# Four groups of products per step of a gated recurrence, with two shared PSUM banks in turn

## The chip, the cores and the metric

The kernel runs on one core of a Trainium2 chip. The metric is the device time of one execution in microseconds (us); smaller is better. The median of three runs of the kernel before is 412.56 us, the lowest 410.94, the highest 412.81.

## What is computed

A gated linear recurrence over 768 tokens for 4 batches of 8 heads, each 48 wide, is followed by a mixture of experts with one expert per token:

```python
f = 1.0 / (1.0 + np.exp(-f_logit))
for t in range(S):
    state = f[:, :, t, :, None] * state + np.einsum('bhd,bhe->bhde', k[:, :, t], v[:, :, t])
    y[:, :, t] = np.einsum('bhd,bhde->bhe', q[:, :, t], state)
x = y.transpose(0, 2, 1, 3).reshape(B * S, H * D)     # 3072 rows of 384
logits = x @ w_gate                                   # 8 experts
expert_idx = np.argmax(logits, axis=1)
gate_w = softmax(logits)[expert_idx]
out = gate_w * (relu(x @ w1[expert_idx]) @ w2[expert_idx])   # 384 -> 1024 -> 384
```

## The kernel before

The recurrence is computed in chunks of 128 tokens. A unit is one chunk of two batches (16 heads); there are 12 units, and units of the same parity follow one another in time for the same pair of batches. Everything is in float32. For each unit, `steps` (L446, lines 452 and 455) computes the log decays from f with Exp and Ln on ScalarE, `total` (L457) takes their running sum with a scan on VectorE, `growth` (L471) and `decay` (L485) take Exp of it with both signs on ScalarE, `by_r` (L478) multiplies the keys on GpSimd and `by_decay` (L497) the queries on VectorE.

On TensorE a unit then needs seven groups of products, which the loop over n at L721 writes out by hand, as a software pipeline over three units. In step n, with `here` = n, `back` = n - 1 and `last` = n - 2:

- `score(here, 0)` and `score(here, 1)` (L505): keys times queries, two heads side by side on 64 partitions each. `copy_predicated` on VectorE (L515) keeps the causal part.
- `keys(here)` (L517), between the two: turns the keys by products with the identity (tile kp), which `keep` (L527) copies to kn on ScalarE.
- `rows(last)` (L603): turns the results into rows and computes the logits in the same products (tile xp), reduced on VectorE (lg, L628). `settle` (L595) has copied those results out of yt, `lay` (L638) copies the rows on ScalarE, and waits for the reduction of the same bank.
- `within(back)` (L531): masked scores times v, accumulated in yt; `before(back)` (L546): the state times the queries, in the same yt.
- `added(here)` (L567): kn times v (tile dp), which `update` (L583) adds to the state on VectorE; GpSimd multiplies by the decay in the step after. Units 10 and 11 have no `added`, as nobody uses their state.

Every second step a group of two units is routed (class `Route`, L195): `choose` picks the expert on VectorE, `count` (L218) makes two products (tile rp), `place` (L223) turns the counts into rows of the sorted store xs in the next step, `weigh` and `fill` compute the gate and `send` scatters the rows with GpSimd's DMA queue.

The order of each engine's instructions is the order in which this code issues them (`manual_schedule`, L652); so each engine's queue, SyncE's with the loads included, goes in program order. [...]three for scores (pss), two for yt, and three (pst) which kp, xp, dp and rp share; the function `turns` (L413) names the bank for each so that each use has two or more uses of other banks ahead of its reuse. The first unit's step n = 0 has an order of its own (L744 to L768), with products of zeros (`warm`) that keep TensorE busy. Loads of k, q, v and f are issued at the end of each step, two to five units ahead. The buffer of f has two places, so f of unit u + 2 can only be loaded when `steps(u)` has read the place. In step 1 `load_first_pads` (L363) writes zeros to 288 rows of xs. In steps 8 and 10 the loads of the first two experts' weights follow.

Behind the recurrence, from step 12 on, the first 128 rows of two experts are read back and worked on while the last units are routed; then all eight experts are worked through (`widen` L295, `narrow` L318). That part is not touched.

Of the kernel before, what the change touches and what calls it, by code (L numbers as in the profile page):

```python
# [10 lines left out]
F32 = mybir.dt.float32  # L11
# [3 lines left out]
OP = mybir.AluOpType  # L15
# [97 lines left out]
def _bc(ap, axis, n):  # L113
    shape = list(ap.shape)
    shape.insert(axis, n)
    return ap[tuple([slice(None)] * axis + [None])].to_broadcast(shape)
# [3 lines left out]
def kernel(  # L120
# [262 lines left out]
    with ExitStack() as st:  # L383
        ld = st.enter_context(tc.tile_pool(name="ld", bufs=1))
        wk = st.enter_context(tc.tile_pool(name="wk", bufs=2))
        pss = st.enter_context(tc.tile_pool(name="pss", bufs=3, space=PSUM))
        psy = st.enter_context(tc.tile_pool(name="psy", bufs=1, space=PSUM))
# [20 lines left out]
        units = [{} for _ in range(NU)]  # L408
        states = [None, None]

        had, used = {"xp0": 0, "xp1": 1, "dp": 2, "rp": None}, [0, 1, 2]

        def turns(what, shape, steady=True):  # L413

            counts = had["rp"] is not None
            b = used[0]
            if steady:
                b = {
                    "kp0": had["dp"] if counts else had["xp0"],
                    "kp1": had["xp1"],  # L420
                    "xp0": had.get("kp0", 0),
                    "xp1": had["rp"] if counts else had.get("kp1", 1),
                    "dp": had.get("kp1", 1) if counts else had["dp"],
                    "rp": had["xp0"],
                }[what]
            had[what] = b
            if what == "dp":
                had["rp"] = None
            used.remove(b)
            used.append(b)  # L430
            return pst.tile(shape, F32, name=what, tag=f"tr{b}")

# [44 lines left out]

        def by_r(u, part=whole):  # L478
            k = units[u]["k"][:, part]
            nc.gpsimd.tensor_tensor(k, k, units[u]["r"][:, part], op=OP.mult)  # L480

# [23 lines left out]
        def score(u, a):  # L505
            x = units[u]
            x["at"] = scores[u % 2]
            ps = [pss.tile([128, HP, C], F32, name="s") for h in range(2)]
            for p, h, r in heads():
                s = HP * a + p  # L510
                nc.tensor.matmul(  # L511
                    ps[h][:, p], lhsT=x["k"][r, s], rhs=x["q"][r, s], start=True, stop=True
                )
            for h in range(2):
                nc.vector.copy_predicated(x["at"][:, a, h], _bc(causal, 1, HP), ps[h])  # L515

        def keys(u):  # L517
            x = units[u]
            x["kn"] = wk.tile([128, SEG, C], F32, name="kn", bufs=1)
            x["kp"] = []  # L520
            for a in range(2):
                kp = turns(f"kp{a}", [128, HP, C], u < NU - 2)
                for p in range(HP):
                    nc.tensor.transpose(kp[:, p], x["k"][:, HP * a + p], ident)  # L524
                x["kp"].append(kp)
# [69 lines left out]
        def settle(u):  # L595
            x = units[u]
            x["ys"] = wk.tile([128, 2, HP, C], F32, name="ys", bufs=1)
            for a in range(2):
                nc.scalar.copy(x["ys"][:, a], x["yt"][:, a])

        group = {}

        def rows(u):  # L603

# [11 lines left out]
            for a in range(2):  # L616
                j = 2 * (u - g[0]) + a
                xp = turns(f"xp{a}", [128, HP, XW], u < NU - 4)
                for p in range(HP):
                    nc.tensor.matmul(  # L620
                        xp[:, p],
                        lhsT=x["ys"][:, a, p],
                        rhs=wx[:, p, 0:XW] if a else wx[:, p, E:WX],
                        start=True,
                        stop=True,
                    )
                gate = slice(0, E) if a else slice(2 * D, XW)
                nc.vector.reduce_sum(  # L628
                    group["lg"][:, j],
                    xp[:, :, gate].rearrange("p h e -> p e h"),  # L630
                    axis=AX_X,
                )
                x["xp"].append(xp)
# [26 lines left out]
        for i in (1, 0):  # L660
            nc.gpsimd.memset(scores[i], 0.0)
        warmth = pst.tile([128, C], F32, name="warmth", tag="tr2")

        def warm(count):

            for _ in range(count):
                nc.tensor.matmul(warmth, lhsT=pad[:, 0:C], rhs=pad[:, 0:C], start=True, stop=True)  # L667

# [6 lines left out]
        for part in ab:  # L675
            growth(0, part)
            by_r(0, part)
            decay(0, part)
            by_decay(0, part)
# [18 lines left out]
        def narrow_early(x, w):  # L698
            narrow(x, 0, w, turns("yp", [128, DM], False), None)

# [19 lines left out]
        sends, later, decayed = [], None, None  # L720
        for n in range(NU + 2):  # L721
            here, back, last = n, n - 1, n - 2
            rt = None
            if here < NU:
                units[here]["old"] = states[here % 2]
            if 0 <= last:
                settle(last)
            if here < NU:
                score(here, 0)
            if 0 < n and n + 1 < NU:  # L730
                by_r(n + 1)
                ends(n + 1)
            if later:
                settled(*later)
                later = None
            if decayed:
                decayed()
                decayed = None
            if sends:
                now = sends if n >= NU - 1 else sends[:1]  # L740
                for send in now:
                    send()
                del sends[: len(now)]
            if n == 0:  # L744
                warm(2)
                keys(0)
                warm(4)
                for part in ab:
                    total(1, part)
                for part in ab:  # L750
                    growth(1, part)
                    by_r(1, part)
                    decay(1, part)
                    by_decay(1, part)
                    if part == ab[0]:
                        score(0, 1)
                warm(8)
                ends(1)
                last_decay(1)
                keep(0)  # L760
                steps(2)
                load(4, "f")
                load_consts()
                load_gate()
                load(3, "k")
                total(2)
                steps(3)
                growth(2)  # L768
            elif here < NU:
                if n == 1:  # L770
                    added(0)
                    decayed = update(0)
                keys(here)
                keep(here)
                score(here, 1)
            if 0 < n and n + 2 < NU:
                total(n + 2)
            if 0 <= last:
                rt = rows(last)
                if rt:  # L780
                    rt.choose()
            if 0 < n and n + 1 < NU:
                decay(n + 1)
                last_decay(n + 1)
            if 0 < n and n + 3 < NU:
                steps(n + 3)
            if 0 <= last:
                lay(last)
            if rt:
                rt.weigh()  # L790
            if 0 < n and n + 2 < NU:
                growth(n + 2)
            for a in range(2):
                if 0 <= back < NU:
                    within(back, a)
            if n == NU + 1:
                widen(soon[0], weights[0], early_h, range(3, 7))
            if n == NU:
                for x in soon:
                    turn_early(x)  # L800
            if 0 <= back < NU:
                before(back)
            if 0 < n and n + 1 < NU:
                for part in ab:
                    by_decay(n + 1, part)
            if n == 1:
                decayed()
            if 0 < here < NU and here // 2 < NC - 1:
                added(here)
                decayed = update(here)  # L810
            if rt:
                rt.count(turns("rp", [128, 2, rt.n, E], n < NU - 2))
                later = (n, rt)
                if n >= NU:
                    settled(*later)
                    later = None
# [3 lines left out]
            if n == NU + 1:  # L820
                widen(soon[0], weights[0], early_h, range(7, NF))
            if 0 < n and n + 3 < NU:
                load(n + 3, "k")
# [4 lines left out]
            if n == 1:  # L828
                load_first_pads()
            if n + 5 < NU:  # L830
                load(n + 5, "f")
# [72 lines left out]
        def check(okc, over):  # L904
            op = turns("op", [128, 1], False)
            nc.tensor.matmul(op, lhsT=const("ones"), rhs=okc, start=True, stop=True)
# [302 lines left out]
```

## Time and profile before

The profile is of one execution on the chip. A row of a timeline holds its start, its length, engine, line, operation, output and inputs, their sizes and how many instructions were merged; in square brackets stands how long the engine was idle ahead of it and what ended that. A float32 product shows as two instructions. PEclk is the granted clock of TensorE as a share of full clock.

| | before |
|---|---|
| median of three runs | 412.56 us |
| profiled execution | 411.07 us |
| its span, first to last instruction | 409.2 us |
| TensorE busy | 395.6 us (97%) |
| VectorE, ScalarE, GpSimd busy | 161.1, 106.0, 113.0 us |
| mean granted clock | 0.991 |
| start of step 2, 3, 10, 11 (first score) | 27.95, 35.91, 102.16, 110.89 us |
| first product of step 12 | 118.96 us |
| expert loop begins | 149.58 us |

### The profile page before, as it was taken

Reading aid. Unit: us, or ns where it says so; the run is one execution under the profiler, and the core shown is the slowest. Engines: PE = TensorE matmul, PEld = TensorE weight load, DVE = VectorE, ACT = ScalarE, POOL = GpSimd, SP = SyncE. Lnnn points to the kernel's source line nnn. Section 1 sums busy time; section 2 is a strip of 40 time slices with the busy share of each in tenths; the row PEclk is TensorE's granted clock in tenths of the full one; section 3 lists DMA queues with packets and bytes.
Section 4 is the critical chain, followed back from the end, with each engine's and each line's share of the span. In section 5 each row is a group of like instructions: output and inputs, shape, how many; then the busy total and the mean of one; then the engine's idle time right before and its main releaser. Section 6 shows DMA issues by size and latency. Waiting matters only on the chain.

```text
span 409.2 us, 7342 instructions
## 1 busy us (share of the span) xinstructions
PE 395.6 (97%) x2906; PEld 276.6 (68%) x2906; DVE 161.1 (39%) x342; ACT 106.0 (26%) x196; POOL 113.0 (28%) x120
## 2 busy tenths in 40 slices
PE   8989999999999999999999999999999999999991
PEld 8879898898889767675555555545555555554640
DVE  6898888888655532131121131122113113111110
ACT  6887877766442000000000000010010010011000
POOL 6477386869706200101001001001100100100010
PEclk9989999999999999999999999999999999999998
DMA  7969877759953469493469999990081489993000
GB/s 281 360 213 378 323 265 240 239 192 358 400 159 113 152 187 325 88 340 63 166 220 344 388 393 270 375 301 20 33 301 38 96 296 388 404 398 135 20 29 15
DMA packets 52122, 95.22 MB, mean 233 GB/s; under 512 B 21440, under 2 KB 41333, under 8 KB 50032
## 3 DMA queue, kind: packets, MB, share of 16 engines
q1 hardware_dynamic: 48592, 84.96, 61.4%
q0 software_dynamic: 3200, 9.64, 6.4%
q8 instruction: 24, 0.39, 0.4%
q10 hardware_dynamic: 288, 0.08, 0.2%
q14 instruction: 18, 0.15, 0.1%
HBM read 79.65 MB, written 15.40 MB: 232 GB/s over the span
## 4 chain that ended last, share of the span: by engine, by line
PE 92%; ACT 2%; DVE 2%; POOL 1%; issue 0%; POOLq 0%; ACTq 0%; DVEq 0%
PE yps L320 28%; PE hps L304 28%; PE xp L620 6%; PE s L511 5%; PE yt L537 5%; PE s L304 3%; PE yps L1009 3%; PE hps L981 3%; PE yp L320 3%; PE yt L558 3%; PE kp L524 2%; PE dp L574 2%; PE warmth L667 2%; DVE sum L462 1%; ACT r L476 1%; POOL rend L483 1%
## 5 line engine op out<-in xcount | busy, mean ns | idle before, releaser
L320 PE MATMUL yps<-w2t,hT 128*128 128x384 f32 x352 | 115.9, 487 | 0.0
L304 PE MATMUL hps<-xT,w1t 128*128 128x384 f32 (+1 forms) x384 | 115.0, 460 | 0.7 <-DVE ysb L331 0.7
L304 PEld LDWEIGHTS hps<-xT,w1t 128*128 128x128 f32 x384 | 72.9, 190 | 42.1 <-DVE ysb L331 1.3
L320 PEld LDWEIGHTS yps<-w2t,hT 128*128 128x128 f32 x352 | 66.4, 190 | 47.5 <-issue 2.9
L183 POOL DMA_INDIRECT out_dram<-ysb,dst x26 | 25.3, 974 | 240.4 <-DVE ysb L331 240.4
L314 ACT ACTIVATE hT<-hps 128x384 f32<-128x384 f32 (+1 forms) x28 | 14.2, 506 | 203.2 <-PE hps L304 203.2
L316 DVE TENSOR_SCALAR hT<-hps 128x384 f32<-128x384 f32 (+1 forms) x28 | 16.2, 577 | 98.2 <-PE hps L304 98.2
L331 DVE TENSOR_SCALAR ysb<-yps,tg 128x384 f32<-128x384 f32 x22 | 13.6, 618 | 87.7 <-PE yps L320 87.7
L183 POOL DMA_INDIRECT xs<-xr,posi x24 | 32.4, 1349 | 26.6 <-DVE counts L227 12.0
L515 DVE COPY_PREDICATED at<-mpack,s 128x512 f32<-128x512 uint8 x48 | 32.4, 728 | 12.2 <-PE s L511 12.2
L480 POOL TENSOR_TENSOR k<-k,r 128x1024 f32<-128x1024 f32 (+1 forms) x14 | 30.1, 2156 | 22.1 <-ACT r L476 22.0
L511 PE MATMUL s<-q,k 64*128 64x128 f32 x384 | 28.8, 285 | 2.3 <-DVE at L515 1.4
L462 DVE TENSOR_TENSOR_SCAN sum<-g,cap 128x1032 f32<-128x1032 f32 (+1 forms) x14 | 28.4, 2032 | 3.2 <-ACT g L455 3.2
L511 PEld LDWEIGHTS s<-q,k 64*128 64x128 f32 x384 | 23.9, 187 | 5.6 <-DVE at L515 2.6
L537 PE MATMUL yt<-at,v 128*48 128x128 f32 x384 | 25.1, 287 | 0.0
L620 PE MATMUL xp<-fpack,ys 128*128 128x104 f32 x192 | 24.2, 279 | 0.8 <-ACT g L488 0.6
L620 PEld LDWEIGHTS xp<-fpack,ys 128*128 128x128 f32 x192 | 22.3, 191 | 2.2 <-ACT g L488 0.8
L537 PEld LDWEIGHTS yt<-at,v 128*48 128x48 f32 x384 | 21.9, 129 | 1.2
L500 DVE TENSOR_TENSOR q<-q,g 128x512 f32<-128x512 f32 x24 | 17.9, 783 | 0.5 <-DMA q<-in_qu_dram 0.3
L529 ACT COPY kn<-kp 128x512 f32<-128x512 f32 x24 | 13.0, 602 | 5.2 <-PE kp L524 5.2
L452 ACT ACTIVATE g<-f 128x1024 f32<-128x1024 f32 (+1 forms) x14 | 13.2, 941 | 4.5 <-DMA f<-in_fu_dram 4.5
L288 DVE STREAM_TRANSPOSE xT<-xrow 128x1152 f32<-128x1152 f32 (+2 forms) x10 | 14.3, 1432 | 0.0
(106 smaller groups left out, 319.0 us busy)
## 6 DMA issues: line engine op xcount, KB each, us to landing
qw<-in_moe_w_dram SPq DMA_DIRECT2D x16, 1536.0 KB, 15.5
w1t<-in_moe_w_dram SPq DMA_DIRECT2D x8, 1536.0 KB, 7.6
w2t<-in_moe_w_dram SPq DMA_DIRECT2D x8, 1536.0 KB, 15.7
k<-in_ku_dram SPq DMA_DIRECT2D x12, 512.0 KB, 4.7
q<-in_qu_dram SPq DMA_DIRECT2D x12, 512.0 KB, 5.5
f<-in_fu_dram SPq DMA_DIRECT2D x11, 512.0 KB, 6.4
xs<-pad SPq DMA_DIRECT2D x8, 600.0 KB, 4.1
v<-in_vu_dram SPq DMA_DIRECT2D x12, 384.0 KB, 4.6
```

Source lines behind the costliest of these rows:

```text
L183: ins = nc.gpsimd.indirect_dma_start(out=dst, out_offset=bass.IndirectOffsetOnAxis(ap=idx, axis=0), in_=src, in_offset=None, bounds_check= ...
L288: nc.vector.transpose(x["xT"].rearrange("p k (i c) -> p i k c", c=BK), x["x"].rearrange("p i (r k) -> p i k r", k=KD),)
L304: nc.tensor.matmul(x["h"][:, f], lhsT=w[0][:, j, b * 128 : b * 128 + 128], rhs=x["xT"][:, j], start=j == 0, stop=j == KD - 1,)
L316: nc.vector.tensor_scalar(to, x["h"], 0.0, None, op0=OP.max)
L320: nc.tensor.matmul(yp, lhsT=x["hT"][:, f, t * C : t * C + C], rhs=w[1][:, f, :], start=f == 0, stop=f == NF - 1,)
L462: nc.vector.tensor_tensor_scan(x["sum"][:, part].rearrange("p s c -> p (s c)"), x["g"][:, part].rearrange("p s c -> p (s c)"), cap[:, part ...
L480: nc.gpsimd.tensor_tensor(k, k, units[u]["r"][:, part], op=OP.mult)
L500: nc.vector.tensor_tensor(q, q, x["dec"][:, part], op=OP.mult)
L511: nc.tensor.matmul(ps[h][:, p], lhsT=x["k"][r, s], rhs=x["q"][r, s], start=True, stop=True)
L515: nc.vector.copy_predicated(x["at"][:, a, h], _bc(causal, 1, HP), ps[h])
L537: nc.tensor.matmul(x["yt"][DP * (h ^ a) : DP * (h ^ a) + D, a, p], lhsT=x["v"][:, a, 2 * p + h], rhs=x["at"][:, a, h, p], start=p == 0, st ...
L620: nc.tensor.matmul(xp[:, p], lhsT=x["ys"][:, a, p], rhs=wx[:, p, 0:XW] if a else wx[:, p, E:WX], start=True, stop=True,)
```

## The change

Each step's products are put in another order, so that groups of the same shape are neighbours: both scores; then the turned keys, the counts of the step before and the rows; then the products with v and the added keys; then the state. Scores have four banks; kp, xp with the counts, and dp take two banks in turn. The masks follow all four scores. Decays of the next unit go ahead of the copies of keys, `weigh` ahead of the scores of the next step, `by_decay` behind the rows as one instruction, and place and fill behind that. Units 10 and 11 have no turned keys. Step 0 is written out ahead of the loop: the keys of unit 0 are multiplied on VectorE, all scores of unit 0 come before its turned keys, the products of zeros go to yt, `steps(3)` is in step 1 behind `by_decay(2)`, and f of unit 5 is loaded behind the pads in step 1. From step 11 on, `place` stands between the counts and the rows and the scatters follow at once. The diff, cut to its core:

```diff
-        pss = st.enter_context(tc.tile_pool(name="pss", bufs=3, space=PSUM))
+        pss = st.enter_context(tc.tile_pool(name="pss", bufs=4, space=PSUM))
...
-        def turns(what, shape, steady=True):
...
-            return pst.tile(shape, F32, name=what, tag=f"tr{b}")
+        used = [0, 1]
+
+        def turns(what, shape):
+
+            used.append(used.pop(0))
+            return pst.tile(shape, F32, name=what, tag=f"tr{used[-1]}")
...
-        def by_r(u, part=whole):
+        def by_r(u, part=whole, on=nc.gpsimd):
             k = units[u]["k"][:, part]
-            nc.gpsimd.tensor_tensor(k, k, units[u]["r"][:, part], op=OP.mult)
+            on.tensor_tensor(k, k, units[u]["r"][:, part], op=OP.mult)
...
-            for h in range(2):
-                nc.vector.copy_predicated(x["at"][:, a, h], _bc(causal, 1, HP), ps[h])
+
+        def mask(u, a, h):
+            x = units[u]
+            nc.vector.copy_predicated(x["at"][:, a, h], _bc(causal, 1, HP), x["ps", a][h])
...
+        def pair():
+
+            xp = turns("xp", [128, 512])
+            w = HP * XW
+            counts = xp[:, w : w + 2 * 4 * E].rearrange("p (two n e) -> p two n e", two=2, e=E)
+            return xp[:, 0:w].rearrange("p (h w) -> p h w", h=HP), counts
...
-                xp = turns(f"xp{a}", [128, HP, XW], u < NU - 4)
+                xp = first if first is not None and a == 0 else pair()[0]
...
-                nc.tensor.matmul(warmth, lhsT=pad[:, 0:C], rhs=pad[:, 0:C], start=True, stop=True)
+                nc.tensor.matmul(yt[:, 0, 0], lhsT=pad[:, 0:C], rhs=pad[:, 0:C], start=True, stop=True)
...
-            by_r(0, part)
+            by_r(0, part, nc.vector)
...
+        score(0, 0)
+        score(0, 1)
+        keys(0)
+        warm(13)
+        mask(0, 0, 0)
+        for part in ab:
+            total(1, part)
+        for a, h in ((0, 1), (1, 0), (1, 1)):
+            mask(0, a, h)
+        for part in ab:
+            growth(1, part)
+            by_r(1, part)
+        for part in ab:
+            decay(1, part)
+            by_decay(1, part)
+        ends(1)
+        last_decay(1)
+        steps(2)
+        total(2)
+        keep(0)
+        growth(2)
+        load(4, "f")
+        load_consts()
+        load_gate()
+        load(3, "k")
+        load(2, "v")
+        load(3, "q")
+
+        for n in range(1, NU + 2):
             here, back, last = n, n - 1, n - 2
+            ahead = n + 1 < NU
+            state = n < NU - 2
...
             if 0 <= last:
                 settle(last)
+            if later and later[0] < NU - 1:
+                later[1].weigh()
             if here < NU:
-                score(here, 0)
-            if 0 < n and n + 1 < NU:
+                for a in range(2):
+                    score(here, a)
+            if ahead:
                 by_r(n + 1)
                 ends(n + 1)
...
+            if ahead:
+                decay(n + 1)
+                last_decay(n + 1)
+            if n == 1:
+                units[0]["old"] = None
+                added(0)
+                update(0)()
+            if state:
                 keys(here)
                 keep(here)
-                score(here, 1)
-            if 0 < n and n + 2 < NU:
+            if here < NU:
+                for a in range(2):
+                    for h in range(2):
+                        mask(here, a, h)
+            if n == 1:
+                by_decay(2)
+                steps(3)
+            if n + 3 < NU:
+                steps(n + 3)
+            if n + 2 < NU:
                 total(n + 2)
+            bank = None
+            if later:
+                bank, counts = pair()
+                later[1].count(counts[:, :, 0 : later[1].n])
+                if n >= NU - 1:
+                    settled(*later)
+                    later = None
+                    scatter_some(n)
             if 0 <= last:
-                rt = rows(last)
...
+                rt = rows(last, bank)
                 lay(last)
+            if 1 < n and ahead:
+                by_decay(n + 1)
             if rt:
-                rt.weigh()
-            if 0 < n and n + 2 < NU:
+                rt.choose()
+                if n >= NU - 1:
+                    rt.weigh()
+            if later:
+                settled(*later)
+                later = None
+            if n + 2 < NU:
                 growth(n + 2)
             for a in range(2):
-                if 0 <= back < NU:
+                if back < NU:
                     within(back, a)
...
-            if 0 <= back < NU:
-                before(back)
...
-            if 0 < here < NU and here // 2 < NC - 1:
+            if state:
                 added(here)
                 decayed = update(here)
+            if back < NU:
+                before(back)
             if rt:
-                rt.count(turns("rp", [128, 2, rt.n, E], n < NU - 2))
                 later = (n, rt)
                 if n >= NU:
+                    rt.count(turns("rp", [128, 2, rt.n, E]))
                     settled(*later)
                     later = None
...
             if n == 1:
                 load_first_pads()
+                load(5, "f")
             if n + 5 < NU:
                 load(n + 5, "f")
```

## The prediction

> **What bounds the kernel now.** I read the page first (TensorE busy 97% of a 409.2 us span, 92% of the chain of waits), then the windows by stage, then the timelines of one step. The recurrence, where the change lies, ends near 125 us; after it two matrix products per expert run at full clock and are not touched. Windows, columns: span, busy PE, PEld, DVE, ACT, POOL, clock, DMA share, GB/s.
>
> ```profile
> 19.93:23.34 3.42, 2.04 (x23) 1.56 (x22) 3.42 (x5) 3.01 (x6) 0.61 (x1) 1.00 0.57 228
> 23.34:26.76 3.41, 3.41 (x36) 3.41 (x37) 3.41 (x3) 3.32 (x5) 3.41 (x2) 0.50 0.34 59
> 35.91:102.16 66.25, 66.25 (x1085) 59.55 (x1081) 57.70 (x123) 48.41 (x88) 47.44 (x47) 1.00 0.80 280
> ```
>
> Steps 3 to 9 take 66.25 us and TensorE is never idle, but VectorE is at 87% of it: a step has room for little waiting between the two. Ahead of it, TensorE is idle 40% of one window and at half clock in the next. One step, from the timelines:
>
> ```profile
> 45.62 1.16 PE L511 MATMUL s<-q,k 64*128 64x128 f32 x16
> 46.71 1.09 PE L524 MATMUL kp<-fpack,k 128*128 128x128 f32 x8
> 47.73 1.16 PE L511 MATMUL s<-q,k 64*128 64x128 f32 x16
> 48.83 2.03 PE L620 MATMUL xp<-fpack,ys 128*128 128x104 f32 x16
> 50.79 1.96 PE L537 MATMUL yt<-at,v 128*48 128x128 f32 x32
> 52.67 1.09 PE L558 MATMUL yt<-q,state 48*48 48x128 f32 x32
> 53.69 1.14 PE L574 MATMUL dp<-v,kn 128*64 128x48 f32 x32
> 54.76 1.16 PE L511 MATMUL s<-q,k 64*128 64x128 f32 x16
> ...
> 47.40 1.07 ACT L529 COPY kn<-kp 128x512 f32<-128x512 f32 x2 [1.07 <-PE kp L524]
> ...
> 48.06 0.72 DVE L227 COPY counts<-fpack 128x8 f32<-128x8 f32 x1
> 48.69 0.18 DVE L228 COPY counts<-rp 128x32 f32<-128x32 f32 x1
> 48.90 0.24 DVE L229 TENSOR_TENSOR_SCAN sums<-fpack,counts 128x40 f32<-128x40 f32 x1
> 49.17 0.21 DVE L239 TENSOR_TENSOR place<-rp,sums 128x32 f32<-128x32 f32 x1
> ...
> 51.48 2.29 DVE L462 TENSOR_TENSOR_SCAN sum<-g,cap 128x1032 f32<-128x1032 f32 x1
> 53.68 0.26 DVE L628 TENSOR_REDUCE lg<-xp 128x8 f32<-128x32 f32 x2
> 53.86 1.28 DVE L500 TENSOR_TENSOR q<-q,g 128x512 f32<-128x512 f32 x2
> ```
>
> Seven groups, 9.14 us (9.70 with the two count products rp)[...]. The copy of turned keys starts 0.69 after the first turn. In the first units it is the loads that matter:
>
> ```profile
> 27.17 0.43 SPq L442 DMA_DIRECT2D f<-in_fu_dram  x1
> ...
> 29.40 0.93 SPq L366 DMA_DIRECT2D xs<-pad  x2
> ...
> 32.90 1.06 ACT L452 ACTIVATE g<-f 128x1024 f32<-128x1024 f32 x1 [1.14 <-DMA f<-in_fu_dram]
> ```
>
> The first line is the load of f for unit 5, issued ahead of the pads; ScalarE already waits 1.14 us for it, and the DMA runs at 347, 377 and 327 GB/s in 27 to 36 us, share 1.0: it has no room.
>
> [...] score pairs start 0.112 apart, but 0.21 lies before the first of the next group, and its second pair comes late by 0.04 to 0.10: 0.13 to 0.20 per boundary. [...] f5 above took 5.7 us. [...]
>
> **The change, part by part.** Times in a step are from its first score.
>
> *Merged groups.* Gone per step: one score boundary (0.20), one between turns and rows (0.17), one between the products with v and the added keys (0.13): 0.5 us. The last stands whole.
>
> *Two banks in turn.* A step takes five: kp, kp, xp, xp, dp. So xp's first half (with the counts ahead of it) takes the bank of the first kp and must wait for its copy. Scores end at 1.99 (1.09 and eight more pairs at 0.112); the first kp is complete and ScalarE starts at +0.69, a copy takes 0.59, a wake-up 0.05: xp starts 1.34 after kp, where it would have started at 0.93. The wait of 0.41 eats the second saving and the first. All of PE is queued behind it. Step: 1.99 + 1.34 + 1.96 (xp) + 2.81 (1.88 with v, plus 16 pairs of dp at 0.058) + 1.03 (state) = 9.13, against 9.14. Bounds of the wait: 0 and 0.6, if ScalarE, which has settle and decay before it (done at 2.3), comes late.
>
> dp takes the bank of xp's first half. In steps without counts it waits for the copy of those rows: VectorE masks from 1.19 (four at 0.62), scan to 5.9, reduction, ScalarE's copy to 6.75; dp is due at 7.1, so this is hidden by 0.3. In steps 4, 6 and 8 the counts lie in that bank, and place reads them only after by_decay (L500): 5.9 + 0.2 + 1.28 = 7.4, then L227 0.63, L228 0.21, L229 0.27, L239 0.21: 8.65. dp was due at 7.55. State products, the next scores and so all of the next step stand behind it. Such a step is 8.65 + 1.03 + 1.02 = 10.7; with L227 at the 0.17 that other rows have, 10.2. I take 10.6. Steps 3 to 9: 4 x 9.14 + 3 x 10.6 = 68.4, against 66.25: **+2.1** (bounds -0.5 and +3).
>
> *Last keys not turned.* Step 10 was 8.73 (102.16 to 110.89): without kp 1.02, a boundary 0.20 and a stall of 0.62 there, and with two counts for 0.55, 7.45. Step 11, 8.07, loses 1.02 and 0.20: 6.85. **-2.5**. The early rows, read back after the scatters, come later relative to step 11 (four scatters in it in place of two, 1.28 each), but their turn is due 13 us after its start and done about 12.3; without that cover it costs up to 1.5.
>
> *First units.* by_r(0) goes to VectorE: 4 x 0.67 from 8.0, ready at 10.7; before, the two engines side by side needed 3.40 and 2.98 and ended at 11.31. Warming writes yt, so waits for its memset (3.27, not 1.24); 48 products, the first cold at 0.213, end at 10 to 12, not 9.1. The first mask stands ahead of unit 1's scans, so those start at 12.0 to 13.7 against 12.47. I take nothing, bounds -0.9 and +1.7. Two steps of exp/ln (L452, L455; 2.2 each) move behind kn, not ahead.
>
> *The load of f5* is the large one. steps(3) moved into step 1, so f5 can only follow it, and is put behind k4, v3, q4 and the pads: 512 + 384 + 512 + 450 KB = 1.90 MB, at 350 to 370 GB/s 5.2 us. It was used at 32.90 and is now at 38.1. ScalarE keeps its order: exp and ln of unit 5 (2.15), then the row copies of unit 0, and now dp of unit 2 waits for these through its bank. 38.1 + 2.15 + 0.46 + 0.05 = 40.75; dp 1.03; step 3 starts at 41.8, not 35.91: **+5.9** (bounds +4.5 and +7.5). TensorE is idle in between, so a window at half clock over step 3 is as likely as not: up to 1.7, I take **+0.8**.
>
> Sum: 5.9 + 0.8 + 2.1 - 2.5 = +6.3. The profiled execution took 411.07 for its span of 409.2; that gives 417.4. The median of the runs shown is 1.5 higher (412.56), which gives 418.9. I say 418.
>
> **Rivals.** (1) *The load is hidden.* If f5 lands by 34 all the same (issue order is against it, 1.9 MB lie ahead), only -2.5 + 2.1 is left: 412. (2) *Faster: the two banks don't bind.* Place: the hand-over of kp's bank to xp and of xp's to dp. If the copy of keys ends within 0.93 of the first turn and place reads counts before dp is due (7.55), each step saves its 0.5 (7 x 0.5 = 3.5), and with -2.5 and a first part no later the kernel takes 406.5. For it: VectorE is busy 87%, not all; against it: 0.69 + 0.59 is already over 0.93. From an early loss below 6 it decides the sign. (3) *The clock falls in the steps.* Steps 4, 6 and 8 idle 1.1 and 0.4 us; if one window at 34% idle suffices (40% did, 0.62 in 3.41 did not), each costs 1.7 more: 423.
>
> **Chances.** Forecast 0.62, (1) 0.12, (2) 0.12, (3) 0.14. The range of 411 to 423 leaves out (2) and the upper part of (3). Within 0.5% (2 us) is what a measurement of this kernel can't tell from no change. Faster 0.13, same 0.11, slower 0.76.
>
> **What would show it.** Right: exp of unit 5 starts near 38 after a DMA wait; step 3 starts near 42; xp waits for kn about 0.4 in each step to 9; dp waits about 1.1 for place in three steps and nowhere else; steps 10 and 11 near 7.4 and 6.9. Wrong: step 3 starts by 37, or steps without counts take 8.7.

## The result, and the profile after

The changed kernel takes 422.29 us (median of 4 runs, 421.56 to 423.23); the kernel before took 412.69 in its 4 runs beside it. The ratio is 1.0244, 95% interval 1.0209 to 1.0278: slower by 9.6 us. The profiled execution took 423.23, the slowest of the four, with a span of 421.2 against 409.2. So the traces explain 12.0 us, a little more than the medians differ. In e11 below, three of eight executions, the profiled one among them, ran longer at a lower granted clock (420.75 to 421.30 us at 0.975 to 0.979, the others 413.86 to 418.11 at 0.987 to 0.996); its ratio leaves them out. By stage, from the first scores of steps 3 and 10 and the first product of step 12:

| stage | before | after | difference | forecast |
|---|---|---|---|---|
| start to step 3 | 35.91 | 43.97 | +8.06 | +5.9 |
| steps 3 to 9 | 66.25 | 70.03 | +3.78 | +2.1, and +0.8 for the clock |
| steps 10 and 11 | 16.80 | 14.15 | -2.65 | -2.5 |
| step 12 to the end | 290.28 | 293.05 | +2.8 | 0, up to +1.5 |

Four places in the trace carry this. First the windows by stage (columns as in the prediction: span, busy PE, PEld, DVE, ACT, POOL, clock, DMA share, GB/s):

```profile
27.49:30.91 3.42, 1.78 (x18) 1.19 (x15) 3.42 (x5) 2.81 (x4) 0.72 (x1) 1.00 0.93 313
30.91:37.74 6.83, 5.19 (x30) 4.99 (x32) 5.23 (x6) 2.08 (x4) 4.92 (x6) 0.50 1.01 366
37.74:41.15 3.41, 1.16 (x22) 0.90 (x17) 0.00 (x0) 1.68 (x3) 0.00 (x0) 1.00 0.93 351
41.15:47.98 6.83, 5.89 (x66) 5.58 (x67) 2.08 (x4) 4.20 (x8) 3.42 (x4) 0.50 0.52 184
43.97:114.00 70.03, 65.89 (x1078) 60.22 (x1076) 64.39 (x113) 47.27 (x83) 44.60 (x45) 0.97 0.64 218
```

Before, TensorE was busy for the whole of steps 3 to 9; now it is idle for 4.14 us of them, and VectorE's busy time has grown from 57.70 to 64.39 us for the same work. Twice ahead of step 3 a window with TensorE idle (48% and 66%) is followed by two at half clock. The timeline there shows the load and who waits:

```profile
30.68 3.06 SPq L426 DMA_DIRECT2D f<-in_fu_dram  x2
...
39.44 1.06 ACT L436 ACTIVATE g<-f 128x1024 f32<-128x1024 f32 x1 [6.45 <-DMA f<-in_fu_dram]
...
41.58 0.46 ACT L643 COPY xr<-xp 128x384 f32<-128x384 f32 x1
...
42.09 1.95 PE L560 MATMUL dp<-v,kn 128*64 128x48 f32 x32 [3.19 <-ACT xr L643]
```

f of unit 5, the first of the two loads in the first row, is issued at 30.68 instead of 27.17 and used at 39.44 instead of 32.90. The copy of the rows stands behind its exponential on ScalarE, and the product dp behind that copy. One step with counts (step 6), from the timeline:

```profile
73.11 2.35 POOL L464 TENSOR_TENSOR k<-k,r 128x1024 f32<-128x1024 f32 x1 [2.09 <-ACT r L460]
73.14 2.37 DVE L212 TENSOR_TENSOR oh<-fpack,val 128x32 f32<-128x32 f32 x1
74.17 2.06 PE L495 MATMUL s<-q,k 64*128 64x128 f32 x32
76.04 2.57 DVE L501 COPY_PREDICATED at<-mpack,s 128x512 f32<-128x512 uint8 x4
76.16 1.09 PE L510 MATMUL kp<-fpack,k 128*128 128x128 f32 x8
...
77.48 0.41 PE L220 MATMUL xp<-oh,fpack 128*128 128x32 f32 x2 [0.24 <-ACT kn L515]
...
80.90 1.21 DVE L484 TENSOR_TENSOR q<-q,g 128x1024 f32<-128x1024 f32 x1
...
82.60 0.21 DVE L239 TENSOR_TENSOR place<-xp,sums 128x32 f32<-128x32 f32 x1
...
82.91 1.14 PE L560 MATMUL dp<-v,kn 128*64 128x48 f32 x32 [1.06 <-ACT r L460]
```

The counts start 1.32 after kp, as forecast (1.34). dp starts 0.10 after L239 has ended; the profile names ScalarE's r, which ended in the same moment, but in steps 4, 6 and 8 alike the distance to L239 is 0.10, and e2 below tests it. And there is a line I had not expected: L212, 32 numbers per partition, takes 2.37 us where it took 0.19 before. It begins with GpSimd's L464 and ends with it. The masks (L501) behind it begin 1.87 after the step's first score, against 1.19 in step 5. Last, the early rows behind step 12:

```profile
125.60 0.98 POOL L183 DMA_INDIRECT xs<-xr,posi  x1 [0.31 <-issue]
...
131.47 1.76 SPq L267 DMA_DIRECT2D xrow<-xs  x4
...
136.31 0.69 DVE L288 STREAM_TRANSPOSE xT<-xrow 128x384 f32<-128x384 f32 x1 [3.29 <-DMA xrow<-xs]
...
137.06 3.73 PE L304 MATMUL s<-xT,w1t 128*128 128x128 f32 x18 [1.93 <-DVE xT L288]
```

The last scatter is issued 2.5 us ahead of step 12's first product (128.15); before it was 7.3 ahead, and the turn waited for no DMA. Now VectorE waits 3.29 for the rows and TensorE 1.93, and its 18 products then run for the most part at half clock (0.50 from 136.73 to 140.14, behind a window with TensorE idle 47%): 3.73 instead of 2.25.

### The profile page after: what moved, and what is told of

The parts are those of the page before. It is cut to its first block, busy times and chain, and to the rows that moved or that the text cites. A ratio compares the mean times of both kernels' runs of the same rounds, so it can differ in the third digit from the quotient of the medians.

```text
span 421.2 us, 7296 instructions
## 1 busy us (share of the span) xinstructions
PE 394.1 (94%) x2888; PEld 277.1 (66%) x2888; DVE 168.9 (40%) x334; ACT 104.7 (25%) x192; POOL 106.8 (25%) x118
## 4 chain that ended last, share of the span: by engine, by line
PE 79%; DVE 7%; DMA 4%; ACT 4%; issue 3%; SPq 1%; POOL 1%; POOLq 0%; DVEq 0%; ACTq 0%
PE yps L320 27%; PE hps L304 27%; PE s L495 4%; PE s L304 3%; PE yps L1025 3%; PE hps L997 3%; PE yp L320 2%; PE xp L613 2%; DVE at L501 2%; PE dp L560 2%; DVE sum L446 2%; DMA f<-in_fu_dram 2%; PE yt L523 2%; PE yt L544 2%; PE yt L658 2%
## 5 line engine op out<-in xcount | busy, mean ns | idle before, releaser
L464 POOL TENSOR_TENSOR k<-k,r 128x1024 f32<-128x1024 f32 (+1 forms) x12 | 26.4, 2200 | 39.0 <-ACT r L460 35.6
L501 DVE COPY_PREDICATED at<-mpack,s 128x512 f32<-128x512 uint8 x48 | 31.1, 720 | 6.3 <-PE s L495 4.5
L183 POOL DMA_INDIRECT xs<-xr,posi x24 | 27.8, 1159 | 20.8 <-DVE sums L229 12.4
L613 PE MATMUL xp<-fpack,ys 128*128 128x104 f32 x192 | 25.9, 291 | 4.3 <-ACT kn L515 3.4
L495 PE MATMUL s<-q,k 64*128 64x128 f32 x384 | 26.4, 291 | 2.1 <-POOL rend L467 2.1
L613 PEld LDWEIGHTS xp<-fpack,ys 128*128 128x128 f32 x192 | 24.0, 203 | 5.7 <-ACT kn L515 4.6
L523 PE MATMUL yt<-at,v 128*48 128x128 f32 x384 | 24.2, 280 | 0.0
L560 PE MATMUL dp<-v,kn 128*64 128x48 f32 x320 | 11.9, 231 | 5.7 <-ACT xr L643 3.2
L585 ACT COPY ys<-yt 128x512 f32<-128x512 f32 x24 | 12.9, 589 | 17.3 <-PE yt L544 17.3
L560 PEld LDWEIGHTS dp<-v,kn 128*64 128x64 f32 x320 | 11.3, 146 | 6.7 <-ACT xr L643 3.4
```

The lines of the kernel that those rows point to most:

```text
L183: ins = nc.gpsimd.indirect_dma_start(out=dst, out_offset=bass.IndirectOffsetOnAxis(ap=idx, axis=0), in_=src, in_offset=None, bounds_check= ...
L464: on.tensor_tensor(k, k, units[u]["r"][:, part], op=OP.mult)
L495: nc.tensor.matmul(ps[h][:, p], lhsT=x["k"][r, s], rhs=x["q"][r, s], start=True, stop=True)
L523: nc.tensor.matmul(x["yt"][DP * (h ^ a) : DP * (h ^ a) + D, a, p], lhsT=x["v"][:, a, 2 * p + h], rhs=x["at"][:, a, h, p], start=p == 0, st ...
L560: nc.tensor.matmul(x["dp"][r, s], lhsT=x["kn"][:, s, r], rhs=x["v"][:, a, 2 * p + h], start=s == 0, stop=True, skip_group_check=True,)
L613: nc.tensor.matmul(xp[:, p], lhsT=x["ys"][:, a, p], rhs=wx[:, p, 0:XW] if a else wx[:, p, E:WX], start=True, stop=True,)
```

## The experiments

Theory: the late load, the place held by two banks, and the early rows each cost what the trace shows. Rivals: the load hurts only with shared banks, or not at all; VectorE, not the banks, sets the steps. "Ratio" is to the kernel before on the same chip: 412.1 us for e1 to e4, 416.65 for e5 to e8 (another chip), 412.2 for e9 to e11, 412.3 for e12. The changed kernel has 1.0244.

**e1, f5 loaded first.**

```diff
+            if n == 1:
+                load(5, "f")
             if n + 3 < NU:
                 load(n + 3, "k")
...
                 load_first_pads()
-                load(5, "f")
```

> The kernel after, with the load of f for unit 5 moved ahead of k for unit 4 in step 1; nothing else. Theory (the load of f5 behind 1.9 MB is what delays the first units): Exp of unit 5 at about 34 instead of 39.4, step 3 at about 38 to 39 instead of 44.0, total about 5 to 7 us less, 415.5 to 417. Rival (ScalarE's order and the half clock are what is late, the load only fills a gap): Exp of unit 5 earlier, but step 3 not before 42, total 420 or more.

Measured: 416.11 us (415.52 to 417.97), ratio 1.0118 [1.0082, 1.0155]. The exponential of unit 5 starts at 33.60, step 3 at 38.70 instead of 43.97. The place of one load is worth 6.2 us by the medians and 5.2 by the ratios (0.0126 of 412), so over half of the loss.

**e7, the same order in the kernel before**, with all else as it was:

```diff
             if n == 1:
                 load_first_pads()
-            if n + 5 < NU:
+                load(5, "f")
+            if 0 < n and n + 5 < NU:
                 load(n + 5, "f")
```

> The kernel before, with the single edit that the load of f5 in step 1 goes behind k4, v3, q4 and the first pads in SyncE's queue, as in the changed kernel; the seven groups of products, three banks in turn and the first units' order stay. Theory A (the late load is enough: the exponential of unit 5 waits for f5 until 37 to 39 us, and with it the decay, lay and settle work behind it on ScalarE): step 3 starts 3 to 6 us later, with a half-clock window, and the time is 415.5 to 418.5, ratio 1.008 to 1.015. Rival B (the late load hurts only together with two shared banks, since lay is what lets the next bank go): step 3 starts less than 1.5 us later and the time is 412 to 413.5.

Measured: 423.89 against 416.65 us, ratio 1.0183 [1.0130, 1.0237]. Step 4 starts at 52.31 instead of 45.62 and step 10 is 7.0 later. From its timeline:

```profile
39.17 1.06 ACT L452 ACTIVATE g<-f 128x1024 f32<-128x1024 f32 x1 [7.53 <-DMA f<-in_fu_dram]
...
41.83 1.97 PE L524 MATMUL kp<-fpack,k 128*128 128x128 f32 x8 [4.70 <-ACT xr L650]
```

With three banks in turn it is kp instead of dp that waits for the row copies behind the exponential. So the load alone is enough, and the rival that it needs two banks falls. The 6.7 us at step 4 happen to equal the 5.9 + 0.8 of the forecast, which was made for step 3 of the changed order. The loss is above the 1.008 to 1.015 expected, and it comes one step later than expected: step 3 itself starts at 35.97.

**e2, dp in the other bank** in units 4, 6 and 8:

```diff
+            if u in (4, 6, 8):
+                used.append(used.pop(0))
             x["dp"] = turns("dp", [128, SEG, D])
```

> The kernel after, with the added keys (dp) of steps 4, 6 and 8 in the bank of the second rows tile, not in the one that holds the counts. Theory (dp waits for place because the counts share its bank): dp starts about 8.0 after the step's first score in steps 4, 6 and 8 where it started 8.06, 8.74 and 8.71, so these steps take 10.15, 10.2 and 10.1 at most and the total falls by 1 to 2.5. Rival (VectorE is behind, since small operations stand still while GpSimd multiplies keys, and takes the next step's masks late whatever bank dp has): the stall moves to the next scores or masks and the total changes by less than 0.7.

Measured: 420.51 us, ratio 1.0207 [1.0180, 1.0235]. Steps 4, 6 and 8 take 9.55, 10.10, 10.21 instead of 10.14, 10.83, 10.81; the steps after 6 and 8 grow from 9.10 to 9.38. The held bank costs 0.6 to 0.7 in each of these steps, of which steps 7 and 9 give back 0.28, so about 1.4 us from step 4 to step 10. It is not the whole of the excess: with it gone steps 6 and 8 are still 0.6 above step 4, as the rival had it.

**e3, turned keys in the banks of scores** from unit 3 on:

```diff
-                kp = turns("kp", [128, HP, C])
+                if u < 3:
+                    kp = turns("kp", [128, HP, C])
+                else:
+                    kp = pss.tile([128, HP, C], F32, name="s")
```

> The kernel after, with the turned keys of units 3 to 9 in two of the four score banks instead of the two banks in turn. Theory (merging groups is worth 0.5 us a step, and the wait of the rows for the copy of the keys eats 0.4 of it): rows start 0.93 after the first turn instead of 1.33, steps without counts take 8.7 instead of 9.1, total 2 to 3 us less. Rival ([...]scores now wait for the copies): steps stay at 9.1, total within 0.7.

Measured: 423.30 us, ratio 1.0292 [1.0252, 1.0331]. In total a miss, as 2 to 3 us less were expected. Steps without counts do fall to 8.78, the 0.3 that the wait for kn took away. But steps 4, 6 and 8 rise to 11.0 to 11.1: kp now waits 0.8 to 0.9 for the masks, which are late where VectorE stood still in L212 (2.36). So four groups can save time, but in the steps with counts VectorE is in the way; e12 tests that.

**e4, the kernel before without the last keys:**

```diff
-                keys(here)
-                keep(here)
+                if here < NU - 2:
+                    keys(here)
+                    keep(here)
                 score(here, 1)
```

> The kernel before, with nothing changed but that the keys of units 10 and 11 are neither turned nor copied. Theory (step 10 loses a group, two boundaries and the wait for the decay copies' order on ScalarE, step 11 a group): steps 10 and 11 take 7.5 and 6.9 in place of 8.73 and 8.07, and as the early rows are not read later than before the total falls by 1.5 to 2.5, to about 410.5. Rival (the scatters and the rows read back set the time of step 12, not TensorE): total within 0.7 of 412.7.

Measured: 410.46 us, ratio 0.9978 [0.9959, 0.9996]. Step 10 falls from 8.73 to 7.93 and widening starts 1.06 earlier. Here the gain is 1 us, not the 1.5 to 2.5 expected nor the 2.65 of the changed kernel: the scores of the last steps wait twice 0.6 us for the masks of the bank that they reuse, waits that the changed kernel, with four banks for scores, does not have there.

**e6, GpSimd's product in quarters**, for units 5 to 11:

```diff
-            k = units[u]["k"][:, part]
-            on.tensor_tensor(k, k, units[u]["r"][:, part], op=OP.mult)
+            for i in range(0, SEG, 2) if u > 4 else (None,):
+                p = part if i is None else slice(i, i + 2)
+                k = units[u]["k"][:, p]
+                on.tensor_tensor(k, k, units[u]["r"][:, p], op=OP.mult)
```

> The changed kernel, with GpSimd's product of keys and growth (L464) of units 5 to 11 issued as four instructions over 256 columns instead of one over 1024. Theory A (a small VectorE instruction that falls into such a GpSimd instruction stands still until it ends): the longest of L212 and L253 goes from 2.4 and 1.9 us to about 0.6, the masks of steps 6 and 8 come 0.5 to 0.65 us sooner, these steps go from 10.8 to 10.15 or 10.4, and the time to 420.5 to 421.8. Rival B (their length has another cause, such as the wait for a semaphore counted as busy time): the two lines still show 1.9 to 2.4 us and the time stays within 0.5 us, 422 to 423. Rival C (splitting costs GpSimd more than it frees VectorE): L464 together takes 2.8 us and more instead of 2.36, the decays by which keys and queries are ready come later and the time is 423 to 425.

Measured: 426.10 against 416.65 us, ratio 1.0211 [1.0147, 1.0274], which does not tell it from the changed kernel. The steps do. Its timeline:

```profile
73.53 2.79 POOL L466 TENSOR_TENSOR k<-k,r 128x256 f32<-128x256 f32 x4 [2.10 <-ACT r L460]
73.56 0.74 DVE L212 TENSOR_TENSOR oh<-fpack,val 128x32 f32<-128x32 f32 x1
```

L212 now takes 0.74, one quarter of GpSimd's work, not 2.37, and L253 0.27 instead of 1.90. Steps 6 and 8 take 10.16 instead of 10.82, like step 4. Theory A holds; the quarters cost GpSimd 0.43 per unit.

**e5, places between counts and rows already in step 10:**

```diff
-                if n >= NU - 1:
+                if n >= NU - 2:
```

> The changed kernel, with the early rows' places taken one step sooner: from step 10 on the places are written between the counts and the product rows, and the scatters sent there, where the changed kernel does that from step 11 on and in step 10 still takes the places behind by_decay. Theory (the 2.8 us lost behind step 12 are a chain that begins with places taken late): the rows of the early tokens reach memory about 2 us sooner, so the first early rows are read back before the turn wants them; the TensorE stall of 1.93 us before L288 and VectorE's wait of 3.29 us for the rows are gone, so is the half-clock window at 136.7; the widening starts 6.2 to 7 us after step 12's first product instead of 8.9. Time 419.5 to 420.5 us, ratio to the kernel before 1.017 to 1.021. Rival (the rows are late because the DMA that gathers them waits for the transfer queue or its own time, and places have time to spare): the stall stays between 1.5 and 2 us and the time at 422 to 423. A cost is possible either way: step 10 itself may become 0.3 to 0.7 us longer, since the counts hold the first rows bank until the places are read.

Measured: 426.99 against 416.65 us, ratio 1.0254 [1.0207, 1.0302]. A miss in the total: the early rows do come in time (widening starts 6.8 us after step 12's first product, not 8.9), but step 10 takes 11.63 instead of 7.30. The places stand behind four masks on VectorE, so the rows wait 2.6 us for their bank, and half clock follows: the products of the rows take 3.59 instead of 2.03, and the page shows a granted clock of 0.8 to 0.9 from 116.6 to 127.2. The last early scatter comes at 125.16, hardly sooner than 125.60, and step 12 starts 4.2 later (132.32).

**e8, e1 with e2 and e5.**

> The changed kernel with three edits at once: the load of f5 ahead of k4 in step 1, the state product dp of units 4, 6, 8 in the bank that doesn't hold the counts, and the places taken between counts and rows from step 10 on. If each is a cost of its own the gains add up: from 422.3 by 6.2, 1.8 and 2 to 412.0 to 413, ratio 0.998 to 1.002 against the kernel before. If the edits share a cost (with the load early, ScalarE's order at steps 1 and 2 remains the limit, and the places' lateness is taken up by the same wait), it is 413.5 to 415. If better than 410.5 the four groups are worth more than the step-by-step tally says.

Measured: 421.54 against 416.65 us, ratio 1.0119 [1.0072, 1.0166], as e1 alone. The gains did not add up as expected. Steps 4 to 9 are 1.4 us shorter than in e1, but step 10 takes 12.04, and step 3 starts 2.2 later than in e1, behind a granted clock of 0.6 to 0.7 from 31.5 to 41.9 us on its page, as much as two windows at half clock give; in e1 it was about one (the products with v of step 2 took 3.25 instead of 1.96). On this chip VectorE also stands still in step 13, for 4.80 us in e5 and 4.57 in e7, and ScalarE for 4.75 and 5.74; the trace says only that the releaser was remote. The pages of all four runs on it, e5 to e8, have 1% of their chain under "another core or an unknown queue", which the changed kernel's page does not have, so these four are compared by their steps and by the ratio.

**e9, choice and places ahead of by_decay in every step**, on top of e1:

```diff
-            if 1 < n and ahead:
-                by_decay(n + 1)
             if rt:
                 rt.choose()
...
                 later = None
+            if 1 < n and ahead:
+                by_decay(n + 1)
```

> The changed kernel with the load of f5 ahead of k4 in step 1, and with choice and places of a route put ahead of by_decay on VectorE in every step (the changed kernel has them behind it). Theory (the long count steps come from the places' lateness, 1.2 us of by_decay ahead of them and VectorE standing still beside GpSimd's by_r): dp no longer waits for L239, L212 and L253 fall outside by_r and take 0.2 us, steps 4, 6 and 8 go from 10.82 to 9.5 to 9.8, the first early rows come about 1.2 us sooner. Against the kernel with the early load alone (ratio 1.0118) that is 3 to 4.5 us: ratio 1.001 to 1.005. Rival (by_decay, now 1.3 to 1.6 us later, holds the next step's scores): the steps that follow begin with a wait for q, non-count steps grow from 9.10 to 9.5 or more, and the ratio stays above 1.007.

Measured: 420.85 us, ratio 1.0223 [1.0183, 1.0262], against 1.0118 for e1. My theory for this run fell, and the rival's mechanism (scores that wait for by_decay) came, though in the count steps. dp starts 7.51 after the first score, as early as was hoped, but those steps take 11.62:

```profile
58.49 2.36 POOL L464 TENSOR_TENSOR k<-k,r 128x1024 f32<-128x1024 f32 x1 [5.14 <-ACT r L460]
58.63 3.30 DVE L484 TENSOR_TENSOR q<-q,g 128x1024 f32<-128x1024 f32 x1
...
60.79 1.19 POOL L467 COPY rend<-sum 128x8 f32<-128x8 f32 x1
62.08 1.16 PE L495 MATMUL s<-q,k 64*128 64x128 f32 x16 [2.00 <-POOL rend L467]
```

Now by_decay (L484) falls into GpSimd's product: it takes 3.30 instead of 1.22, and the next scores wait for it. (The profile names L467, which ended in the same moment, for once held up by VectorE: 1.19 instead of 0.19.) Not all of the 4.3 us between e9 and e1 is due to this: step 2 takes 14.35 against 12.95 and step 9 10.30 against 9.10, and the mean granted clock of the profiled execution was 0.984 against 0.991. In the changed kernel the order saves by_decay from this and lets L212 and L253 pay.

**e10, e9 with the turned keys of units 2 to 9 in the banks of scores; e11, that with dp in the other bank.**

> The same, and the turned keys of units 2 to 9 in the four banks of scores instead of the two in turn. Theory (four groups are worth what the forecast counted once no bank holds them back, and the loss at step 3 comes from turned keys that wait for dp's bank in step 2): steps without counts 8.8, count steps 9.3 to 9.6, step 2 shorter by 1 us or more; ratio 0.994 to 1.000, that is level with the kernel before or a little faster. Rival (the turned keys now wait for the masks of this step's scores on VectorE, as where that was tried alone): count steps 9.8 or more, and the ratio is within 0.003 of the run without this edit.

> The same again, and dp of units 4, 6 and 8 in the bank that doesn't hold the counts. If places still hold dp in the run before this: count steps 0.3 to 0.6 us shorter and the ratio 0.003 to 0.005 lower. If they come in time there: count steps unchanged or 0.1 to 0.3 longer (dp then waits for the copy of the second rows bank), ratio within 0.002.

Measured: e10 415.23 us, ratio 1.0083 [1.0048, 1.0118]; e11 ratio 1.0090 [1.0050, 1.0130]. Neither forecast for e10 came whole: the ratio fell by 0.014, which the rival excluded, and the count steps stayed where the theory had them gone. Step 2 shrinks from 14.35 to 11.49 (12.95 in e1), as the rows no longer wait there for the copy of turned keys whose bank they shared (2.44 in e9); how much of this is the clock (a mean of 0.982 in the profiled execution, 0.984 in e9) was not separated. Steps 3 and 7, without counts, take 8.79 and 8.74. Count steps stay at 11.62 in both: by_decay still runs beside GpSimd, and the place of dp makes no difference.

**e12, five edits:** e1, turned keys of units 2 to 9 in the banks of scores, e2, e6, and by_decay ahead of choice and places again except in step 10:

```diff
+            if later and n == NU - 2:
+                settled(*later)
+                later = None
             if 1 < n and ahead:
                 by_decay(n + 1)
```

> The changed kernel with five edits: f5 loaded ahead of k4 in step 1; the turned keys of units 2 to 9 in the banks of scores; dp of units 4, 6, 8 in the bank that doesn't hold the counts; GpSimd's product L464 of units 5 to 11 in quarters; choice and places behind by_decay as in the changed kernel, but in step 10 alone the places ahead of it. Theory (VectorE and GpSimd in each other's way make the count steps long, and two banks the rest): with by_decay ahead of GpSimd's product again the scores no longer wait 2.0 us as they do with places ahead in every step, the masks come in time for the turned keys, steps without counts take 8.8 and count steps 9.2 to 9.8, step 3 starts near 38; widening starts under 7.5 us after step 12's first product. Time 408.5 to 412, ratio 0.992 to 1.000. Rival (turned keys in the banks of scores tie the kernel to VectorE's masks whatever GpSimd does): count steps of 10.3 or more, ratio 1.003 to 1.009.

Measured: 408.40 us (407.75 to 409.48, 6 runs), against 412.28: ratio 0.9912 [0.9891, 0.9933]. It beats both kernels and e4. Its window for steps 3 to 9:

```profile
38.33:101.30 62.97, 62.97 (x1080) 58.13 (x1077) 56.53 (x114) 48.73 (x85) 48.08 (x64) 1.00 0.79 277
```

62.97 us instead of 66.25 before and 70.03 in the changed kernel: 8.78 without counts, 9.23 with them. TensorE is never idle in these steps. From e11 to e12 the count steps fall by 2.4 each, 7.2 us together, as much as the ratios differ (7.3). Widening starts 6.8 us after step 12's first product instead of 8.9.

## Why the prediction was right, and where its sizes were off

*Direction and largest term: right.* The largest part of the loss is the load of f5; e1 takes 5 to 6 us away, e7 puts 7 into the kernel before. That f5 would wait for the 1.90 MB issued ahead of it was an assumption of mine; e1 bears it out, where f5 is issued first and its exponential starts at 33.60 instead of 39.44. In size the term was short: +8.06 for +5.9. I let 1.90 MB pass in 5.2 us at the rate of a full window, and the exponential came at 39.44, not 38.1 (1.34 more). The trace of before had the better number: there f5 had landed at 32.80, and the k, v, q and pads issued behind it landed at 39.69, 6.9 us later. Then dp ran at half clock, 1.88 to the next scores instead of 1.03 (0.85 more). 41.8 + 1.34 + 0.85 is the 43.97 of the trace.

*Half clock: under-sized.* I took +0.8 out of "up to 1.7". Step 3, with a mean granted clock of 0.82, takes 10.95 where an undisturbed step without counts takes 9.10: 1.85.

*Merged groups and two banks: right.* 9.10 against 9.13, with the counts or rows starting 1.32 after kp. Of the rivals, "the two banks don't bind" failed just there: e3 shows 8.78 once they don't.

*Steps with counts: the sum right, its parts not.* Without the clock, steps 3 to 9 lost 1.93 (forecast 2.1), but not as I worked it out (my parts add up to 8.70 for the end of place, not 8.65). L227 took 0.17, so step 4 came at my lower value (10.14; forecast 10.2). Steps 6 and 8 came at 10.8 because L212 had stood still and the masks began 0.67 late. I took VectorE's durations from rows of the kernel before and did not ask which of them would newly run beside GpSimd. The L227 of the prediction's own lines, 0.72 us for a copy of 8 numbers, was such a case: it starts inside this operation of GpSimd and ends with it:

```profile
47.91 0.83 POOL L593 TENSOR_TENSOR state<-state,last 128x384 f32<-128x384 f32 x1
```

L212 (2.37 us) and L253 (1.90) end within 0.05 us of L464; L484 in e9 ended 1.08 after L464, near the 1.22 that it takes outside such a product.

*Last keys: right,* -2.65 for -2.5. *First units:* nothing was taken; up to step 2 they gained 2.0 us (25.97 for 27.95), outside the bounds of -0.9 to +1.7. Step 2 gave it back: in e1 kp waits 0.85 there for the bank of dp and the rows 2.43 for kn, and step 3 starts 2.8 late. So part of the +8.06 is a second wait hidden behind that for f5.

*The early rows: the step that failed.* "Their turn is due 13 us after its start and done about 12.3". It came 15.0 after step 11's start (136.31 against 121.30). The last scatter was issued 4.3 after that start, so 12.3 leaves 8.0 us for its rows to land, come back and be turned; it took 10.7. In e9 and e12, with the places earlier in step 10, widening starts 6.8 us after step 12's first product, and from there to the end these kernels are not behind the kernel before (289.9 and 290.1 against 290.28). But the late places alone don't make the 2.8 us. e2 has them as late, its rows came sooner, 8.5 us from the last scatter to the turn, and its widening starts after 7.0 us; this stage lost 0.9. In e1 widening starts as late as 9.3 us, but no half clock follows (its 18 products take 2.27), and the stage lost 1.7. So the late places cost 0.9 to 2.8 us, by how long the rows take to come back and whether the clock falls. Why the rows came sooner in e2 is open. The rival on the clock was wrong in its place: steps 4, 6 and 8 kept full clock (1.00), but step 3 (0.82) and the products behind step 12 (0.50) did not.

*Open:* from e11 to e12 both the quarters and the order of by_decay and places changed; what each is worth was not separated. Why 1.90 MB took 6.9 us and not 5.2 was not followed either. In e12 step 3 still starts 2.4 us later than before, with a wait of 1.4 of dp for the row copies; a still earlier f5 was not tried.

## What to carry to other kernels

When a reordering moves a load, count the bytes that now lie ahead of it in its queue, and follow who stands behind its first user in order: here one line of a load cost 5 to 7 us (e1, e7), more than the reordered products could save. When instructions of VectorE move, check what GpSimd runs at the new time, since an operation of 0.19 us (L212) took 2.37 here. Merged groups paid here only where the banks between them were released in time (e3: 8.78 instead of 9.10 in the steps without counts); test each wait alone, then all of them together, as single repairs (e2, e3, e9) hid behind the next one.

## What the runs showed of the hardware

Some VectorE operations on tiles in SBUF that start inside a GpSimd tensor_tensor end only after it. A tensor_tensor with both inputs in SBUF took 2.37 us instead of 0.19 for 32 numbers per partition (L212) and 3.30 instead of 1.22 for 1024 (L484 in e9); a tensor_scalar of 4 numbers, with one input, took 1.90 instead of 0.17 (L253), and a copy of 8 numbers 0.72 instead of 0.17 (L227 in the kernel before). Others run through it. Late in step 6 a reduction and L253 start inside the same L464:

```profile
82.87 2.37 POOL L464 TENSOR_TENSOR k<-k,r 128x1024 f32<-128x1024 f32 x1 [0.49 <-ACT r L460]
83.06 0.19 DVE L245 TENSOR_REDUCE posi<-place 128x4 int32<-128x32 f32 x1
83.38 1.90 DVE L253 TENSOR_SCALAR su<-su 128x4 f32<-128x4 f32 x1
```

A reciprocal of 4 numbers also took its usual 0.18 inside L464 (L254 in e9), an addition with one input in PSUM 0.56 (L577; 0.54 to 0.55 elsewhere), and the masks, which read their scores from PSUM, 0.71 to 0.73 each (0.70 to 0.75 elsewhere). It goes the other way too: GpSimd's copy of 8 numbers took 1.19 instead of 0.19 beside L484.

In the changed kernel windows of 3.41 us with TensorE idle 48% and 66% were followed by half clock (0.50). The idle share alone does not decide it: this window of e9, idle 55%, was followed by full clock (1.00).

```profile
80.91:84.32 3.41, 1.52 (x26) 1.55 (x28) 2.57 (x3) 1.98 (x3) 2.69 (x4) 1.00 0.80 224
84.32:87.74 3.42, 3.18 (x32) 2.83 (x30) 3.42 (x5) 2.23 (x5) 3.12 (x3) 1.00 0.75 228
```

Step 6 of the changed kernel, with 1.29 us idle in 10.82, kept full clock (1.00 from 73.99 to 84.81).
